# Attention decode step with gradients: pair sums and q and mod matmuls spread over even and odd heads, eight rows of sixteen scaled by ScalarE

## The chip, the cores and the metric

The kernel runs on one core of one Trainium2 chip. The core has four engines that matter here, each with its own instruction stream executed in order: TensorE (PE, with its weight loads shown as PEld), VectorE (DVE), ScalarE (ACT) and GpSimd (POOL); SyncE (SP) and POOL issue the DMAs. The metric is the device time of one execution in microseconds, the median of several runs.

## The reference, cut to what matters

One token goes through a transformer block whose layer norms are modulated by a condition vector `c`, and all gradients are taken. The part that the change touches is the forward attention: 32 heads, each with its own K and V cache of 8192 rows of 192 values.

```python
mod = (_silu(c) @ w_mod).reshape(c.shape[0], 6, 1, -1)
sa, ca, ga, sb, cb, gb = (mod[:, 0].copy(), ..., mod[:, 5].copy())
h = _layernorm(x, axis=-1) * (1 + ca) + sa
...
q = (x @ wq).reshape(B, Sq, Hq, Dh)                       # one query, 32 heads, Dh = 192
scores = jnp.einsum('bhqd,bhkd->bhqk', q, k) * Dh ** (-0.5)
p = _softmax(scores, axis=-1)
o = jnp.einsum('bhqk,bhkd->bhqd', p, v)
return o.reshape(B, Sq, Hq * Dh) @ wo
...
x = x + ga * _A_ref(h, ...)
h = _layernorm(x, axis=-1) * (1 + cb) + sb
x = x + gb * _B_ref(h, ...)                               # a small MLP mixer
```

The outputs are `x` and the gradients with respect to the inputs, among them dK and dV of the full size of the caches (out_2 and out_3), dwq and dwo, and dw_mod.

## The kernel before, in words

The kernel has a forward half and a backward half. The forward half reads K and V of all heads once and computes, besides the attention output, the products that the backward half needs; the backward half reads V again and writes dK and dV. The order of instructions on PE, DVE, ACT and SP is written out by hand (`manual_schedule` over `ORDER`): each engine executes in the order of the source.

**Tiles.** A head's 8192 rows lie on 128 partitions with 64 rows each (`J`). A K or V half (32 rows a partition, 128 x 32 x 192 bf16) is one DMA of 1536 KB. Five K buffers (`KB`) and three V buffers (`VB`) turn round. A quarter has `JQ` = 16 rows a partition.

**The loop** over heads `i` = 0 to 30 is a pipeline of three heads: `x` is head i (its scores), `y` is head i-1 (softmax, scaling of V, most matmuls), `z` is head i-2 (its last quarter and its results). In one turn the code does, in this order:

- DVE finishes the scores of the head before (`dot_sum` of `d1`, L312, and a maximum, L516), then multiplies the first K half by q (`dot_mul`, L297, tile `prod`, one buffer). PE spreads the maximum (`mx`, L520, pool `psB`, one buffer) and executes quarter 3 of `z` (`m_quarter`: lines 378 and 383 into `mp`, line 395 into `op`).
- DVE makes `negm` (L526). ACT computes the exponentials `E4` (L343) and two copies of them (L344, L346).
- DVE halves `prod` by adding its halves (`dot_half`, L302); PE sums the rest (`dot_tree`, L308, tile `dot_ps`).
- Two quarters of V are scaled by the exponentials (`scale_v`). Of the 16 rows of a quarter, DVE scales the first `JQ - NVA` in one operation (L356) and ACT the other `NVA`, one operation each (L363), after a copy of the weights into the last columns (L354). `NVA` is 7. The scaled quarter `vs` has three buffers. PE executes quarters 0 and 1 of `y`.
- Between them ACT takes the results of `z` out of PSUM (`m_out`): `M1` (L414), `mt` (L416) and `osb` (L422).
- In odd turns, PE makes the sums over partitions for the two heads of a pair (`pair_sums`, L432 to L434, fp32 matmuls of one column into `po`, pool `psS`, one buffer) before quarter 1. In turns with i % 4 = 3 it makes the first half of the next four heads' q too (`q_half`, L265, and the copy by ACT, L267).
- DVE multiplies the second K half (L297), adds `mt` (`m_add`, L427), in odd turns makes the normalised output of the pair (`pair_o`, L444 to L448), halves the product, and PE sums it (`dot_tree`).
- Quarter 2 is scaled. In odd turns PE multiplies the pair's output by `wo` (`pair_ao`, L455) and ACT copies the result (`AO`, L557); with i % 4 = 3 the second half of q follows, with i % 4 = 1 the columns of `mod` (`mod_blocks`, L241, ACT L242), as long as there are any. Then PE executes quarter 2, and quarter 3 is scaled.

**Loads.** SP issues each load when its buffer comes free: the next head's K halves after quarters 3 and 1 of earlier heads (L338), V halves after the scaling of a V half (L292), `wo` in odd turns (L211), and w_q (i % 4 = 2) and w_mod (i = 0, 4, 8) into one buffer `w_st` (L205).

The last two heads (lines 594 to 757) have their own code: scores in quarters, the loads of B_w3 and B_w4 (`w4a`, L658), the results of the last pairs, the layer norms and the MLP. The backward half starts after that.

Of the kernel before, what the change touches and what calls it, by code (L numbers as in the profile page):

```python
# [8 lines left out]
FP32 = mybir.dt.float32  # L9
# [11 lines left out]
def kernel(  # L21
# [27 lines left out]
    P = 128  # L49
    D = A_x.shape[-1]  # L50
    _, HQ, S, DH = A_k_cache.shape
# [3 lines left out]
    J = S // P  # L55
    JH = J // 2
    JQ = J // 4
# [9 lines left out]
    MW = DH + 1  # L67
# [5 lines left out]
    V_, A_, T_ = nc.vector, nc.scalar, nc.tensor  # L73
# [9 lines left out]
    psS = ctx.enter_context(tc.tile_pool(name="psS", bufs=1, space=PS))  # L83
# [150 lines left out]

    mod = col(NMB, "mod")

    def mod_blocks(b0, nb, w):
        ps = psS.tile([P, 16], FP32, name="mod_ps", tag="s")
        for b in range(nb):
            for k in range(ND):  # L240
                T_.matmul(ps[:, b : b + 1], lhsT=w[:, k, b * P : (b + 1) * P], rhs=sc_bf[:, k : k + 1], start=(k == 0), stop=(k == ND - 1))  # L241
        A_.copy(out=mod[:, b0 : b0 + nb], in_=ps[:, 0:nb])  # L242

    sa, ca, ga, sb, cb, gb = (mod[:, k * ND : (k + 1) * ND] for k in range(6))
# [4 lines left out]
    nc.sync.dma_start(out=wm_b, in_=wm_v[:, :, 9 * P : 12 * P])  # L249
    MB0 = 12  # L250
    n0, r0 = layernorm(x_c, "ln0")
    mod_blocks(0, 9, wm_a)
    mod_blocks(9, 3, wm_b)
    ha = col(ND, "ha")
    V_.scalar_tensor_tensor(out=ha, in0=ca, scalar=1.0, in1=n0, op0=ALU.add, op1=ALU.mult)
    V_.tensor_tensor(out=ha, in0=ha, in1=sa, op=ALU.add)
# [2 lines left out]

    qs_bc = const.tile([P, QD], BF16, name="qs_bc")  # L260

    def q_half(n, b, w):
        ps = psB.tile([P, 512], FP32, name="q_ps", tag="b")
        for k in range(ND):
            T_.matmul(ps[:, 0:PW], lhsT=ha_bf[:, k : k + 1].to_broadcast([P, P]), rhs=w[:, k, b * PW : (b + 1) * PW], start=(k == 0), stop=(k == ND - 1))  # L265
        lo = n * CW + b * PW
        A_.activation(out=qs_bc[:, lo : lo + PW], in_=ps[:, 0:PW], func=ACT.Copy, scale=SCALE)  # L267

# [22 lines left out]
    def load_v(h, t, v):  # L291
        nc.sync.dma_start(out=v, in_=V_hd[h][:, t * JH : (t + 1) * JH, :])  # L292
        return v

    def dot_mul(src, vec):
        prod = pp.tile([P, JH, DH], BF16, name="prod", tag="prod")
        V_.tensor_tensor(out=prod, in0=src, in1=vec[:, None, :].to_broadcast([P, JH, DH]), op=ALU.mult)  # L297
        return prod

    def dot_half(prod):  # L300
        w = DH // 2
        V_.tensor_tensor(out=prod[:, :, 0:w], in0=prod[:, :, 0:w], in1=prod[:, :, w : 2 * w], op=ALU.add)  # L302

    def dot_tree(prod, psR, w):

        ps = psR.tile([P, JH, TS], FP32, name="dot_ps", tag="d")
        for k in range(0, w, TS):
            T_.matmul(ps, lhsT=ident_bf, rhs=prod[:, :, k : k + TS], start=(k == 0), stop=(k == w - TS))  # L308
        return ps

    def dot_sum(ps, dst):
        V_.reduce_sum(out=dst, in_=ps, axis=AX.X)  # L312
# [7 lines left out]
    KX, KY, KC, KD, KE = (KB[(2 * HQ + k) % NKB] for k in (-4, -5, -3, -2, -1))  # L320
    OB = (VB[1], KY, KE, VB[1], KD)
    OR = (KY, KC, KE, KX, KD)
    NVA = (7 * JQ) // 16
    MO = 256

    def e_rows(t, pool=psS, tag="s"):
# [6 lines left out]
    with tc.tile_pool(name="vs", bufs=3) as vsp, tc.tile_pool(name="ft", bufs=2) as ft, \  # L333
            tc.tile_pool(name="psM", bufs=2, space=PS) as psM, tc.tile_pool(name="psO", bufs=2, space=PS) as psO, \
            tc.tile_pool(name="psR", bufs=2, space=PS) as psR:
        def load_k(h, t):
            kb = KB[(2 * h + t) % NKB]
            nc.sync.dma_start(out=kb, in_=K_hd[h][:, t * JH : (t + 1) * JH, :])  # L338
            return kb
# [68 lines left out]
        def o_out(h, op, es, os_):  # L408
            os_[h] = ft.tile([P, MW], FP32, name="osb")
            A_.activation(out=os_[h][:, DH:MW], in_=es, func=ACT.Copy, scale=32.0)  # L410
            A_.copy(out=os_[h][:, 0:DH], in_=op[:, 0:DH])
# [13 lines left out]
        def m_add(h, mp, mt):  # L425
            t, b = divmod(h, 2)
            V_.tensor_tensor(out=M2[64 * b : 64 * b + 64, t, :], in0=mp[0:64, MO : MO + MW], in1=mt[64:128, :], op=ALU.add)  # L427

        def pair_sum(po, b, os_h):
            rows = slice(64 * b, 64 * b + 64)  # L430
            for k in range(3):
                T_.matmul(po[rows, k : k + 1], lhsT=os_h[:, k:DH:3], rhs=c32[:, 0:1], start=True, stop=True)  # L432
            T_.matmul(po[rows, 3:4], lhsT=c32[:, 0:64], rhs=os_h[:, DH:MW], start=True, stop=True)
            T_.matmul(po[:, 4 + b : 5 + b], lhsT=c32, rhs=os_h[:, DH:MW], start=True, stop=True)  # L434

        def pair_sums(os2):
            po = psS.tile([P, 8], FP32, name="po", tag="s")
            for b in range(2):
                pair_sum(po, b, os2[b])
            return po  # L440

        def pair_o(t, po):
            rz = tcol(3, "rz")
# [7 lines left out]
        def pair_ao(o2, wo_t, pool=psS, tag="s"):  # L451
            ps = pool.tile([P, ND, 2], FP32, name="ao_ps", tag=tag)
            for i in range(ND):
                for k in range(3):
                    T_.matmul(ps[:, i, :], lhsT=wo_t[:, k, i * P : (i + 1) * P], rhs=o2[:, k, :], start=(k == 0), stop=(k == 2))  # L455
            return ps

        w = load_w(wq_v, 0, CW)
        for b in range(2):
            q_half(0, b, w)  # L460
        mb = MB0
        X, os_, wo_l = {0: {"k": [load_k(0, 0), load_k(0, 1)], "v": [load_v(0, 0, VB[0])]}}, {}, {}
        wo_l[0] = load_wo(0)
# [39 lines left out]
        with tc.manual_schedule(engines=ORDER):  # L503
            for i in range(H1):
# [32 lines left out]
                if z is not None:  # L537
                    mt = m_out(i - 2, z["mp"], z["op"], os_)
                early(i, "mid")
                if last:  # L540
                    po = pair_sums((os_.pop(i - 3), os_.pop(i - 2)))
                if i % 4 == 3 and wch is not None:
                    q_half((i + 1) // 4, 0, wch)
                if y is not None:
                    m_quarter(1, y["k"][0], vs1, y["mp"], y["op"])
                nx["k"].append(load_k(i + 1, 1))
                pb = dot_mul(x["k"][1], qh)
                if z is not None:
                    m_add(i - 2, z["mp"], mt)
                if last:  # L550
                    o2 = pair_o(t, po)
                dot_half(pb)
                x["d1"] = dot_tree(pb, psR, DH // 2)
                if y is not None:
                    vs = scale_v(2, y["v"][1], E4, Ef)
                if last:
                    A_.copy(out=AO[:, :, 2 * t : 2 * t + 2], in_=pair_ao(o2, wo_l.pop(t)))  # L557
                if i % 4 == 3 and wch is not None:
                    q_half((i + 1) // 4, 1, wch)
                    wch = None  # L560
                if i % 4 == 1 and wch is not None:
                    mod_blocks(mb, nb, wch)
                    mb += nb
                    wch = None
                if i % 2 == 1:
# [8 lines left out]
                dot_sum(x["d0"], x["S"][:, 0:JH])  # L574
                if y is not None:
                    y["vs"] = scale_v(3, y["v"][1], E4, Ef)
                nx["v"].append(load_v(i + 1, 0, VB[(2 * i + 2) % NVB]))
                early(i, "end")
                if i == H1 - 3:
# [5 lines left out]
                    nc.sync.dma_start(out=w4b[:, 5 * D : 6 * D], in_=w4v[:, 3, :])  # L585
                if i > H1 - 3:
                    dg_part(1)
                if i == H1 - 1:
                    po = psS.tile([P, 8], FP32, name="po", tag="s")
                    pair_sum(po, 0, os_.pop(H1 - 3))  # L590
            assert mb == NMB and wch is None


# [29 lines left out]
            def psr(shape, dtype, name):  # L623
                return psR.tile(shape, dtype, name=name, tag="d")
# [25 lines left out]
            score_tree(0, d1)  # L650
            score_mul(1, 1)
            score_tree(1, d1)
            dot_sum(d0, x["S"][:, 0:JH])
            m_add(H1 - 2, z["mp"], mt)
            o_rows(H1 - 1, vy, op_y, JH, J)
            o_out(H1 - 1, op_y, es, os_)
            w4a = pp.tile([P, 8, D], BF16, name="w4a", tag="prod")
            nc.sync.dma_start(out=w4a, in_=w4v[:, 4:12, :])  # L658
            w3v = [flat(VB[0])[:, k * F : (k + 1) * F] for k in range(4)] + [w3_4]
# [15 lines left out]

            dot_sum(d1, x["S"][:, JH:J])
            mx = row_max(x["S"])
            po_x = psr([P, 8], FP32, "po_x")
            pair_sum(po_x, 0, os_.pop(H1 - 1))
            negm = neg_max(mx)  # L680
            A_.activation(out=E_all[:, H1, :], in_=x["S"], func=ACT.Exp, bias=negm[:, 0:1], scale=1.0)
            op_x = psO.tile([P, 256], FP32, name="op")
            o_rows(H1, x["v"], op_x, 0, J)
            es = e_sum(H1)
            dg_part(1)
            o_out(H1, op_x, es, os_)
            pair_sum(po, 1, os_.pop(H1 - 2))
            o2 = pair_o(TL - 1, po)
            pair_sum(po_x, 1, os_.pop(H1))
            er_t = [e_rows(TL, psB, "b")]  # L690
            ps_ao = pair_ao(o2, wo_l[TL - 1])
            w3t(1)
            o2 = pair_o(TL, po_x)
            A_.copy(out=AO[:, :, 2 * TL - 2 : 2 * TL], in_=ps_ao)
            ps_ao = pair_ao(o2, wo_l[TL], psB, "b")
            aoP = col(ND, "aoP")
            V_.reduce_sum(out=aoP, in_=AO[:, :, 0 : 2 * TL], axis=AX.X)
# [613 lines left out]
```

## Time and profile before

| | us |
|---|---|
| median of 4 runs | 1445.66 |
| lowest and highest run | 1439.58, 1450.1 |
| the profiled execution | 1450.1 |
| its span, first to last instruction | 1448.3 |
| PE, DVE, ACT, POOL busy in the span | 1205.7, 1109.7, 882.4, 138.1 |
| mean granted TensorE clock | 0.715 |
| HBM read and written | 343.58 MB, 225.91 MB |

An engine's busy time is the union of its instructions. The granted clock is the share of TensorE's full clock that the throttle let through. In the forward half (about the first 570 us) it is near 1, and in the backward half 0.55 on average. DMA engines are busy nearly everywhere: the mean over the span is 395 GB/s. A wait is listed as the waiting engine, its line, the releaser, the sum in us, the count and the longest. In the timeline a row is start, duration (us), engine, line, operation, tiles and shapes, count, and in brackets the engine's idle time before it with the releaser.

### The profile page before, as it was taken

To read this page: it belongs to the slowest core of one execution; us is meant where nothing else is said; L and a number is where in the kernel's file an instruction comes from. 1 tells how busy PE (TensorE), PEld (TensorE's weight loads), DVE (VectorE), ACT (ScalarE), POOL (GpSimd) and SP (SyncE) were. 2 spreads that over 40 slices of the span, in tenths; PEclk is the share of its full clock that TensorE was granted. 3 is DMA by queue.
4 is the path that set the end of the run, shared out by engine and by line. 5 is a ranking of instruction groups with operands and counts; after the bars stand their busy time and mean duration, and the time that the engine had idled before them with its cause. 6 is when DMAs were issued, how large, how long until landed. Compare 5 with 4: busy or idle time off the path is not lost.

```text
span 1448.3 us, 29963 instructions
## 1 busy us (share of the span) xinstructions
PE 1205.7 (83%) x12577; PEld 785.7 (54%) x12577; DVE 1109.7 (77%) x1395; ACT 882.4 (61%) x1923; POOL 138.1 (10%) x240
## 2 busy tenths in 40 slices
PE   3999999999999987887888888789887788778884
PEld 1677777777777766544444444444444444444542
DVE  4999999999999996676766676776676676667674
ACT  0777766777777773545555555566566555555654
POOL 0000000000000000121110110111111111111111
PEclk9999999999999997656555555565556555555555
DMA  9999999999999995699999999999999999999997
GB/s 375 404 407 419 408 418 404 401 400 394 403 396 402 412 413 216 232 401 425 420 395 412 417 398 407 412 415 419 395 423 423 396 417 405 403 384 408 391 401 324
DMA packets 77748, 571.96 MB, mean 395 GB/s; under 512 B 8590, under 2 KB 26718, under 8 KB 37294
## 3 DMA queue, kind: packets, MB, share of 16 engines
q1 hardware_dynamic: 51402, 343.59, 58.9%
q0 software_dynamic: 26192, 226.47, 38.0%
q8 instruction: 98, 1.61, 0.4%
q14 instruction: 36, 0.29, 0.0%
q10 hardware_dynamic: 20, 0.00, 0.0%
HBM read 343.58 MB, written 225.91 MB: 393 GB/s over the span
## 4 chain that ended last, share of the span: by engine, by line
PE 38%; DVE 29%; ACT 11%; DMA 11%; issue 9%; POOL 1%; SPq 0%; ACTq 0%; POOLq 0%; DVEq 0%
PE dot_ps L938 16%; DVE prod L297 9%; DMA out_dram<-KB 6%; PE dv_ps L949 6%; DVE pq L929 5%; ACT vs L363 4%; DVE prod L302 4%; PE wT_ps L816 4%; DVE vs L356 3%; PE mp L378 3%; PE dot_ps L308 2%; DVE S_h L312 2%; ACT wT L817 2%; DMA KB<-in_A_k_cache_dram 2%; DMA out_dram<-stg 1%
## 5 line engine op out<-in xcount | busy, mean ns | idle before, releaser
L950 ACT CAST KB<-dv_ps 128x768 bf16<-128x768 f32 x504 | 382.8, 804 | 279.5 <-PE dv_ps L949 278.7
L938 PE MATMUL dot_ps<-pq,ident_bf 128*128 128x256 bf16 x1536 | 363.8, 407 | 63.5 <-DVE pq L929 63.2
L363 ACT ACTIVATE vs<-VB,Ef 128x192 bf16<-128x192 bf16 x840 | 303.2, 442 | 0.0
L938 PEld LDWEIGHTS <-ident_bf 128*128 128x128 bf16 x1536 | 190.1, 135 | 190.7 <-issue 127.9
L949 PE MATMUL dv_ps<-do_r,er_b 1*128 1x192 bf16 x2048 | 223.3, 337 | 56.1 <-ACT KB L950 51.3
L954 DVE TENSOR_TENSOR KB<-qs_bc,dS 128x3072 bf16<-128x3072 bf16 x126 | 220.4, 1750 | 26.2 <-DMA out_dram<-KB 25.8
L929 DVE TENSOR_TENSOR pq<-VB,do_r 128x3072 bf16<-128x3072 bf16 x126 | 220.4, 1749 | 0.0
L297 DVE TENSOR_TENSOR prod<-KB,qs_bc 128x6144 bf16<-128x6144 bf16 x62 | 207.8, 3351 | 9.7 <-DMA KB<-in_A_k_cache_dram 5.2
L949 PEld LDWEIGHTS <-er_b 1*128 1x128 bf16 x2048 | 92.9, 112 | 178.0 <-issue 170.2
L378 PE MATMUL mp<-vs,KB 128*128 128x193 bf16 x1920 | 187.5, 251 | 0.0
L378 PEld LDWEIGHTS <-KB 128*128 128x128 bf16 x1920 | 168.6, 100 | 17.3 <-issue 4.5
L312 DVE TENSOR_REDUCE dP<-dot_ps 128x32 f32<-128x512 f32 x64 | 44.2, 691 | 145.8 <-PE dot_ps L938 145.8
L793 POOL DMA_DIRECT2D er_b<-er_t x64 | 40.9, 639 | 1169.2 <-PE w3T_ps L666 576.4
L308 PE MATMUL dot_ps<-prod,ident_bf 128*128 128x512 bf16 x372 | 94.3, 391 | 45.7 <-DVE prod L302 45.7
L356 DVE TENSOR_TENSOR vs<-VB,E 128x1728 bf16<-128x1728 bf16 x120 | 123.5, 1049 | 0.0
L302 DVE TENSOR_TENSOR prod<-prod 128x3072 bf16<-128x3072 bf16 x62 | 108.6, 1752 | 0.6
L817 ACT COPY wT<-wT_ps 128x1024 bf16<-128x1024 bf16 x84 | 80.8, 962 | 45.1 <-PE wT_ps L816 42.0
L383 PE MATMUL mp<-vs,KB 128*64 128x193 bf16 x1920 | 103.0, 250 | 0.0
L383 PEld LDWEIGHTS <-KB 128*64 128x64 bf16 x1920 | 77.0, 109 | 19.6 <-issue 19.6
L308 PEld LDWEIGHTS <-ident_bf 128*128 128x128 bf16 x372 | 34.7, 99 | 87.2 <-issue 59.2
L1187 POOL DMA_DIRECT2D out_dram<-KB x127 | 68.4, 542 | 42.7 <-ACT KB L950 17.9
L343 ACT ACTIVATE E<-S_h,negm 128x256 bf16<-128x256 f32 x30 | 15.2, 508 | 86.5 <-DVE negm L526 86.5
(333 smaller groups left out, 1020.9 us busy)
## 6 DMA issues: line engine op xcount, KB each, us to landing
VB<-in_A_v_cache_dram SPq DMA_DIRECT2D x125, 1536.0 KB, 11.2
out_dram<-KB POOLq DMA_DIRECT2D x125, 1536.0 KB, 15.0
KB<-in_A_k_cache_dram SPq DMA_DIRECT2D x64, 1536.0 KB, 10.4
wo_st<-in_A_wo_dram SPq DMA_DIRECT2D x30, 480.0 KB, 9.1
w_st<-in_A_wq_dram SPq DMA_DIRECT2D x12, 960.0 KB, 13.4
out_dram<-wo_st POOLq DMA_DIRECT2D x16, 480.0 KB, 19.9
out_dram<-w_st POOLq DMA_DIRECT2D x7, 960.0 KB, 22.8
w_st<-in_w_mod_dram SPq DMA_DIRECT2D x6, 960.0 KB, 20.3
```

The source lines that it names most:

```text
L297: V_.tensor_tensor(out=prod, in0=src, in1=vec[:, None, :].to_broadcast([P, JH, DH]), op=ALU.mult)
L302: V_.tensor_tensor(out=prod[:, :, 0:w], in0=prod[:, :, 0:w], in1=prod[:, :, w : 2 * w], op=ALU.add)
L308: T_.matmul(ps, lhsT=ident_bf, rhs=prod[:, :, k : k + TS], start=(k == 0), stop=(k == w - TS))
L356: V_.tensor_tensor(out=vs[:, 0:n, 0:DH].rearrange("p j (a b) -> p j a b", b=4), in0=v[:, v0 : v0 + n, :].rearrange("p j (a b) -> p j a b", ...
L363: A_.activation(out=vs[:, k, 0:DH], in_=v[:, v0 + k, :], func=ACT.Copy, scale=Ef[:, j0 + k : j0 + k + 1])
L378: T_.matmul(mp[:, 0:MW], lhsT=kb[:, j0 + k, 0:P], rhs=vs[:, k, 0:MW], start=(q == 0 and k == 0), stop=(z and k == JQ - 1), skip_group_chec ...
L383: T_.matmul(mp[p0 : p0 + 64, MO : MO + MW], lhsT=kb[:, j0 + k, P:DH], rhs=vs[:, k, 0:MW], start=False, stop=(z and k >= JQ - 2), skip_grou ...
L929: V_.tensor_tensor(out=pq[:, q], in0=v_l[s][:, q * JQ : (q + 1) * JQ, :], in1=do_of(ht(s)[0])[:, None, :].to_broadcast([P, JQ, DH]), op=AL ...
L938: T_.matmul(ps[:, q * JQ : (q + 1) * JQ, :], lhsT=ident_bf, rhs=pq[:, q, :, k : k + TS], start=(k == 0), stop=(k == DH - TS), skip_group_c ...
L949: T_.matmul(ps[:, b, k * DH : (k + 1) * DH], lhsT=er[p0 : p0 + 1, 2 * m + k, :], rhs=doh[p0 : p0 + 1, :], start=True, stop=True)
L950: A_.copy(out=dV4[:, 2 * q : 2 * q + 2, m * PW : (m + 1) * PW], in_=ps[:, :, 0:PW])
L954: V_.tensor_tensor(out=dK[:, lo:hi, :].rearrange("p j (a b) -> p j a b", b=4), in0=qh.rearrange("p (a b) -> p a b", b=4)[:, None, :, :].to ...
```

## The change

`NVA` becomes 8: ACT scales eight rows of each quarter, and DVE eight (nine before). The pair sum of a head is executed once per head, after quarter 1 of the turn, and written into spare columns (200 to 207) of the `op` tile of the pair's odd head, in place of a tile of its own; in odd turns `pair_o` moves behind `dot_half` and `dot_tree`. The first half of q is made in turns with i % 4 = 3 as before but later, the second half in turns with i % 4 = 0, and mod in turns with i % 4 = 2 (1 before). The matmuls of `pair_ao`, q and mod stay before quarter 2, and ACT's copies of their results are put in a list `late` that is executed after quarter 3 has been scaled. In the last two heads, pair sums, `pair_o`, `pair_ao` and the copy of `AO` for the last pair but one come earlier or later, as the diff shows.

```diff
-    def mod_blocks(b0, nb, w):
+    def mod_mm(nb, w):
         ps = psS.tile([P, 16], FP32, name="mod_ps", tag="s")
...
+        return ps
+
+    def mod_out(b0, nb, ps):
         A_.copy(out=mod[:, b0 : b0 + nb], in_=ps[:, 0:nb])
...
-    def q_half(n, b, w):
+    def q_mm(b, w):
         ps = psB.tile([P, 512], FP32, name="q_ps", tag="b")
...
+        return ps
+
+    def q_out(n, b, ps):
         lo = n * CW + b * PW
         A_.activation(out=qs_bc[:, lo : lo + PW], in_=ps[:, 0:PW], func=ACT.Copy, scale=SCALE)
...
-    NVA = (7 * JQ) // 16
+    NVA = JQ // 2
...
-        def pair_sum(po, b, os_h):
+        def pair_sum(po, b, os_h, start=True):
             rows = slice(64 * b, 64 * b + 64)
             for k in range(3):
-                T_.matmul(po[rows, k : k + 1], lhsT=os_h[:, k:DH:3], rhs=c32[:, 0:1], start=True, stop=True)
+                T_.matmul(po[rows, k : k + 1], lhsT=os_h[:, k:DH:3], rhs=c32[:, 0:1], start=start, stop=start, skip_group_check=True)
...
                 early(i, "mid")
-                if last:
-                    po = pair_sums((os_.pop(i - 3), os_.pop(i - 2)))
-                if i % 4 == 3 and wch is not None:
-                    q_half((i + 1) // 4, 0, wch)
                 if y is not None:
                     m_quarter(1, y["k"][0], vs1, y["mp"], y["op"])
                 nx["k"].append(load_k(i + 1, 1))
+                if z is not None:
+                    po = (z if last else y)["op"][:, 200:208]
+                    pair_sum(po, i % 2, os_.pop(i - 2), start=False)
+                late = []
                 pb = dot_mul(x["k"][1], qh)
                 if z is not None:
                     m_add(i - 2, z["mp"], mt)
+                dot_half(pb)
+                x["d1"] = dot_tree(pb, psR, DH // 2)
                 if last:
                     o2 = pair_o(t, po)
-                dot_half(pb)
-                x["d1"] = dot_tree(pb, psR, DH // 2)
                 if y is not None:
                     vs = scale_v(2, y["v"][1], E4, Ef)
                 if last:
-                    A_.copy(out=AO[:, :, 2 * t : 2 * t + 2], in_=pair_ao(o2, wo_l.pop(t)))
+                    ps_ao = pair_ao(o2, wo_l.pop(t))
+                    late.append(lambda ps=ps_ao, t=t: A_.copy(out=AO[:, :, 2 * t : 2 * t + 2], in_=ps))
                 if i % 4 == 3 and wch is not None:
-                    q_half((i + 1) // 4, 1, wch)
+                    late.append(lambda ps=q_mm(0, wch), n=(i + 1) // 4: q_out(n, 0, ps))
+                if i % 4 == 0 and wch is not None:
+                    late.append(lambda ps=q_mm(1, wch), n=i // 4: q_out(n, 1, ps))
                     wch = None
-                if i % 4 == 1 and wch is not None:
-                    mod_blocks(mb, nb, wch)
+                if i % 4 == 2 and wch is not None:
+                    late.append(lambda ps=mod_mm(nb, wch), lo=mb, n=nb: mod_out(lo, n, ps))
                     mb += nb
                     wch = None
...
                     y["vs"] = scale_v(3, y["v"][1], E4, Ef)
+                for f in late:
+                    f()
                 nx["v"].append(load_v(i + 1, 0, VB[(2 * i + 2) % NVB]))
...
-                if i == H1 - 1:
-                    po = psS.tile([P, 8], FP32, name="po", tag="s")
-                    pair_sum(po, 0, os_.pop(H1 - 3))
...
             score_tree(1, d1)
+            pair_sum(po, 1, os_.pop(H1 - 2), start=False)
             dot_sum(d0, x["S"][:, 0:JH])
             m_add(H1 - 2, z["mp"], mt)
-            o_rows(H1 - 1, vy, op_y, JH, J)
-            o_out(H1 - 1, op_y, es, os_)
...
             mx = row_max(x["S"])
-            po_x = psr([P, 8], FP32, "po_x")
-            pair_sum(po_x, 0, os_.pop(H1 - 1))
+            o_rows(H1 - 1, vy, op_y, JH, J)
+            o2 = pair_o(TL - 1, po)
             negm = neg_max(mx)
             A_.activation(out=E_all[:, H1, :], in_=x["S"], func=ACT.Exp, bias=negm[:, 0:1], scale=1.0)
+            o_out(H1 - 1, op_y, es, os_)
+            ps_ao = pair_ao(o2, wo_l[TL - 1])
+            A_.copy(out=AO[:, :, 2 * TL - 2 : 2 * TL], in_=ps_ao)
+            po_x = psr([P, 8], FP32, "po_x")
             op_x = psO.tile([P, 256], FP32, name="op")
             o_rows(H1, x["v"], op_x, 0, J)
...
             o_out(H1, op_x, es, os_)
-            pair_sum(po, 1, os_.pop(H1 - 2))
-            o2 = pair_o(TL - 1, po)
+            pair_sum(po_x, 0, os_.pop(H1 - 1))
             pair_sum(po_x, 1, os_.pop(H1))
...
-            ps_ao = pair_ao(o2, wo_l[TL - 1])
             w3t(1)
             o2 = pair_o(TL, po_x)
-            A_.copy(out=AO[:, :, 2 * TL - 2 : 2 * TL], in_=ps_ao)
             ps_ao = pair_ao(o2, wo_l[TL], psB, "b")
```

More of the change, by code (lines that the diff above doesn't have):

```diff
@@ L251 @@
     n0, r0 = layernorm(x_c, "ln0")
-    mod_blocks(0, 9, wm_a)
-    mod_blocks(9, 3, wm_b)
+    mod_out(0, 9, mod_mm(9, wm_a))
+    mod_out(9, 3, mod_mm(3, wm_b))
     ha = col(ND, "ha")
@@ L427, in m_add @@
             V_.tensor_tensor(out=M2[64 * b : 64 * b + 64, t, :], in0=mp[0:64, MO : MO + MW], in1=mt[64:128, :], op=ALU.add)
-        def pair_sum(po, b, os_h):
+        def pair_sum(po, b, os_h, start=True):
             rows = slice(64 * b, 64 * b + 64)
             for k in range(3):
[L432 to L436, printed above, removed]
-            po = psS.tile([P, 8], FP32, name="po", tag="s")
-            for b in range(2):
-                pair_sum(po, b, os2[b])
-            return po
+                T_.matmul(po[rows, k : k + 1], lhsT=os_h[:, k:DH:3], rhs=c32[:, 0:1], start=start, stop=start, skip_group_check=True)
+            T_.matmul(po[rows, 3:4], lhsT=c32[:, 0:64], rhs=os_h[:, DH:MW], start=start, stop=start, skip_group_check=True)
+            T_.matmul(po[:, 4 + b : 5 + b], lhsT=c32, rhs=os_h[:, DH:MW], start=start, stop=start, skip_group_check=True)
         def pair_o(t, po):
@@ L459 @@
         for b in range(2):
-            q_half(0, b, w)
+            q_out(0, b, q_mm(b, w))
         mb = MB0
@@ L587 @@
                     dg_part(1)
-                if i == H1 - 1:
-                    po = psS.tile([P, 8], FP32, name="po", tag="s")
-                    pair_sum(po, 0, os_.pop(H1 - 3))
             assert mb == NMB and wch is None
```

## The prediction

> **What bounds the kernel now.** I first read busy time by stretch. Columns: stretch; its length; busy us of PE, PEld, DVE, ACT, POOL, with instruction counts; granted PE clock; DMA share; GB/s.
>
> ```profile
> 108.00:180.00 72.00, 67.21 (x988) 52.13 (x988) 67.24 (x62) 53.12 (x169) 0.00 (x0) 0.98 1.01 413
> 324.00:396.00 72.00, 66.40 (x956) 51.23 (x957) 67.99 (x64) 51.55 (x164) 0.00 (x0) 0.98 1.00 397
> 600.00:1448.00 848.00, 677.14 (x5039) 381.61 (x5034) 569.87 (x778) 487.41 (x703) 132.07 (x225) 0.55 0.99 403
> ```
>
> The change touches only the forward half (up to about 570 us). There DVE is busy 94% of the time, PE 92 to 93%, ACT 72 to 74%, and the DMA engines always have packets, so at least three resources stand close together. The waits of 72 to 500 us (25 heads) say who sets the pace:
>
> ```profile
> ACT E L343 <- DVE negm L526: 58.3, 25, 4.3
> ACT AO L557 <- PE ao_ps L455: 32.4, 13, 4.6
> ACT qs_bc L267 <- PE q_ps L265: 23.1, 14, 3.1
> DVE rz L444 <- PE po L434: 12.9, 13, 1.2
> DVE S_h L312 <- PE dot_ps L308: 6.3, 6, 1.4
> ```
>
> ACT's waits are long but mostly slack. DVE waits 19 us in all, for PE, nearly all in odd heads; for K tiles it waits 0.3 us. So DVE leads, and loses time to PE in odd heads.
>
> The timeline gives the rest. I count from a head's first `prod` product (L297). Even head 18 starts at 321.93, odd head 19 at 337.83, head 20 at 356.90:
>
> ```profile
> 331.82 0.32 ACT L416 COPY mt<-mp 64x193 f32<-64x193 f32 x1
> 332.38 0.35 DVE L427 TENSOR_TENSOR M<-mp,mt 64x193 f32<-64x193 f32 x1
> 332.76 1.76 DVE L302 TENSOR_TENSOR prod<-prod 128x3072 bf16<-128x3072 bf16 x1
> 333.41 0.52 PE L395 MATMUL op<-vs,ones_bf 128*32 128x193 bf16 x16
> 335.09 2.53 ACT L363 ACTIVATE vs<-VB,Ef 128x192 bf16<-128x192 bf16 x7
> ...
> 347.07 0.69 PE L432 MATMUL po<-c,osb 128*64 128x1 f32 x6
> 349.77 0.18 DVE L444 RECIPROCAL rz<-po 128x3 f32<-128x3 f32 x1 [1.14 <-PE po L434]
> 356.04 0.69 DVE L312 TENSOR_REDUCE S_h<-dot_ps 128x32 f32<-128x512 f32 x1 [1.43 <-PE dot_ps L308]
> ```
>
> Head 18 takes 15.90 us and DVE never stops. Head 19 takes 19.07: DVE waits for both pair sums (1.14), then for a dot tree (1.43) that PE reached late. Heads 18 to 21 take 15.90 + 19.07 + 16.15 + 17.36 = 68.48 us; heads 2 to 29, seven such fours, 477.9.
>
> The late PE is partly a slow PE. Six odd heads (3, 7, 13, 17, 19, 23) hold a stretch like the second line here:
>
> ```profile
> 345.80:349.20 3.40, 3.16 (x53) 2.71 (x51) 2.80 (x2) 2.54 (x8) 0.00 (x0) 1.00 1.04 435
> 349.20:352.60 3.40, 3.40 (x17) 2.46 (x17) 2.79 (x6) 1.21 (x4) 0.00 (x0) 0.50 1.00 417
> ```
>
> The granted clock is 0.50 for 3.4 us, right after a stretch with both pair sums in it. Heads 17 and 13 (half clock) take 18.17, their like without it 17.36; heads 3, 7, 19, 23 take 19.0 to 19.1, their like 17.43 to 17.51. That is 0.8 or 1.6 us an event, 8 us together.
>
> **The change, part by part.**
>
> *One row of 16 from DVE to ACT.* DVE's products cost 1751 ns for 3072 elements and 3351 for 6144: 0.521 ns an element. The quarter's product shrinks from 1728 to 1536 elements, from 1049 to 949 ns: 0.10 us a quarter, 0.40 a head, 12 us over 120 quarters. ACT adds a row: seven take 2.53 us and one alone 0.44, so 0.35 a row, 1.40 a head. The bounds of an added row are 0.35 (queued) and 0.44 (alone); I take 0.35, since the rows are queued.
>
> ACT looks free, but one point is not. DVE's `m_add` (L427) waits for ACT's copy `mt`, which stands behind the first two quarters. In head 18 `mt` is done at +10.21 and DVE's own product before `m_add` at +10.42, so the cover is 0.21. Now `mt` comes 2 x 0.35 later, at +10.91, and DVE is 0.20 earlier, at +10.22. DVE stands still for 0.7 us, and behind `m_add` wait the halving of `prod`, the dot tree, two products and two sums. From `m_add` to the next head it takes 337.83 - 332.38 = 5.45, now 0.20 less. An even head becomes 10.94 + 5.25 = **16.19** us: 0.3 longer than today. Only two of four quarters pay back on DVE, and two rows go onto the path in full.
>
> [...]
>
> *Pair sums, one per head, after the second quarter.* Removed from odd heads: one pair sum (1.1 us of PE, 347.07 to 348.18), the wait for `osb`, and the stand in front of quarter 1. In an even head PE ends quarter 1 at 333.93, +12.0; one pair sum then ends at +13.1. DVE, which now halves `prod` first, comes for `po` at 10.94 + 0.38 + 1.68 = +13.0, so 0.1 to 0.15 of wait is left of 1.14, and the four small `pair_o` operations (0.55) stay. The dot tree follows on PE at +13.1 and takes 1.5; DVE sums it at about +16, so the 1.43 goes. An odd head becomes 16.19 + 0.55 + 0.15 = **16.9**. No stretch of 3.4 us holds two pair sums any more, so I count no half-clock events.
>
> [...]
>
> *q and mod matmuls spread; ACT's `AO`, q and mod copies moved behind the last quarter.* ACT's waits for PE (32.4 + 23.1) go, but they were slack or are priced above. New cost: at every fourth head's turn DVE's first product waits for the q copy. ACT's last quarter ends at 335.09 + 2.53 = +15.69 today, at +17.09 with four rows more; `AO` and q (0.17 and 0.49) end at +17.7. Against +16.9 that is **0.86** once in four heads. The other half of q and mod are read one or more heads later and cost nothing. The copies keep `psB` and `psS` to the head's end: the next `mx` waits for the q copy, but PE reaches it at about +18, after its own matmuls.
>
> *Loads.* SP's order is unchanged. A first K half is issued when PE ends a head's last quarter, today +3.4; ACT's later rows and PE's backlog make that +4.2 to 4.6, which leaves 11.6 to 12 us against 10.2 median (14.5 longest) to landing: hidden on average, and priced by the excess where not. Second K halves go out 4 to 5 us earlier in odd heads. V halves have more than 20 us.
>
> A four without a w_mod load moves 16 x 1.573 (1536 KB) + 2 x 0.49 + 0.98 = 27.1 MB, over 67.04 us 405 GB/s; with one, 28.1 MB, 419. The best 72 us above ran 413, where 28.1 MB take 68. Two fours have it; I add 0.5 us each.
>
> *The end of the forward half.* `pair_o`, `AO` and some matmuls change places. The chain there runs through the landing of `w4a` (issued 553.59, 11.4 us), whose issue hangs on the last score trees, which move little: zero, bounds -1 to +1.
>
> **Sum.** Four heads: 16.19 + 16.90 + 16.19 + 17.76 = 67.04. Seven: 469.3, plus 1.1 for head 29's own extras (18.50 against 17.36), plus 1.0 for loads: 471.4 against 477.9, **-6.5 us**. Half of the removed waits are eaten by the new wait for `mt`. The profiled execution took 1450.1 us (span 1448.3), so 1443.6; it was the slowest of four, whose median is 1445.66. The backward half is untouched, so I shift the median: **1439.2 us**.
>
> **Rivals.**
> - *The new waits do not bind.* If `mt` came in time, DVE alone would need 15.5 + 16.05 + 15.5 + 16.05 = 63.1, and loads would set the pace. At about 418 GB/s the fours take 64.9 (five) or 67.2 (two): 459 + 1.1 against 477.9, some -18, **1428**. Against it: ACT runs without a gap from `E` to `mt` in both heads.
> - *Nothing is left.* A row at 0.44 adds 0.18 to `mt` in each head, 0.36 to a q turn: about 1 us a four; with K half a microsecond late per four, 7 x 1.5 gives +10: **1445 to 1449**.
> - *Slower: half clock in every head.* A pair sum, a dot tree and 15 `ao` or 30 mod matmuls of one or two columns now stand together in each head. If that trips the clock as two pair sums do, 28 heads pay 0.8: +22, less 6.5, **1461**. It decides from about 17 events on (beyond 0.5%). Against it: stretches with 10 of a pair's 20 small fp32 matmuls are not followed by half clock today.
> - *It does not do what it says:* the order of the built program shows eight rows on ACT and the moves as described, so no chance is set aside.
>
> **How the numbers follow.** Forecast 0.5 (own range 1434 to 1444), rival one 0.2, two 0.18, three 0.12. The range holds the first three: 1427 to 1449. Half a per cent (7.2 us, about what a measurement can tell) lies at 1438.4: faster 0.2 and a little under half of 0.5, 0.44; same 0.43; slower 0.13.
>
> **What would show it.** Right: a new DVE wait at `m_add` for ACT's `mt` of about 0.7 us a head; even heads near 16.2, odd near 16.9, every fourth near 17.8, with a wait of the first product for the q copy; `rz` waits near 0.1; no half clock between 72 and 540 us. Wrong: no wait at `mt`; DVE waiting for K tiles more than 5 us in all; clock 0.50 in many heads.

## The result, and the profile after

The changed kernel takes 1441.92 us (median of 43 runs, 1432.17 to 1447.69) against 1446.62 for the kernel before (64 runs beside them): a ratio of 0.9966, 95% interval 0.9954 to 0.9977, or 4.9 us less (3.3 to 6.7). The forecast was 6.5 less. The profiled execution of the changed kernel took 1441.61 us, its span 1439.8.

Busy time by stretch, in the columns of the table shown for the kernel before:

```profile
108.00:180.00 72.00, 67.79 (x1012) 52.04 (x1008) 66.87 (x63) 58.46 (x187) 0.00 (x0) 0.98 1.01 417
324.00:396.00 72.00, 65.74 (x960) 50.44 (x960) 68.04 (x64) 59.72 (x190) 0.00 (x0) 1.00 1.00 406
600.00:1439.00 839.00, 679.56 (x5018) 383.94 (x5015) 567.37 (x777) 486.08 (x702) 131.57 (x224) 0.54 1.00 407
```

ACT's share rose from 72 to 74% to 81 to 83%, DVE's stayed, and the loads run at 406 to 417 GB/s (397 to 413 before). DVE's waits from 72 to 500 us (waiting line, releaser: us in total, times, longest) are of another kind than before:

```profile
DVE M L433 <- ACT mt L422: 11.6, 21, 0.7
DVE prod L303 <- DMA KB<-in_A_k_cache_dram: 5.3, 11, 1.2
DVE prod L303 <- ACT qs_bc L273: 3.1, 6, 0.6
DVE prod L303 <- PE dot_ps L314: 2.0, 2, 1.1
DVE S_h L318 <- PE dot_ps L314: 0.4, 2, 0.3
DVE rz L444 <- PE op L440: 0.4, 2, 0.2
```

Before, DVE stood 19 us for PE in odd heads. Now it stands 2.8 us for PE (2.0 of it for a dot tree, in heads 6 and 10), 11.6 us for `mt`, 5.3 for K tiles (0.3 before) and 3.1 for the q copy. In sum these waits are no shorter than before (22.8 us, 19.5 before); DVE has 0.40 us a head less to do. In the timeline of heads 18 and 19, which start at 319.89 and 336.05 (head 20 at 353.58), the wait at `m_add` is there in both:

```profile
330.81 0.35 DVE L433 TENSOR_TENSOR M<-mp,mt 64x193 f32<-64x193 f32 x1 [0.70 <-ACT mt L422]
...
346.97 0.35 DVE L433 TENSOR_TENSOR M<-mp,mt 64x193 f32<-64x193 f32 x1 [0.70 <-ACT mt L422]
349.20 0.18 DVE L444 RECIPROCAL rz<-op 128x3 f32<-128x3 f32 x1
...
353.58 3.36 DVE L303 TENSOR_TENSOR prod<-KB,qs_bc 128x6144 bf16<-128x6144 bf16 x1 [0.55 <-ACT qs_bc L273]
```

The last line is the new wait for the q copy, and `rz` no longer waits. An undisturbed even head takes 16.17 us, an odd one 16.89, an odd one with a q copy 17.53. Yet heads 2 to 29 together went only from 477.92 to 475.35: 2.6 us, where the sum had 6.5. What the heads show of the cause is in two places. One is head 29, which took 20.90 (18.50 before). Its start, at 503.96, with the half of q that PE makes just before it:

```profile
502.20 0.98 PE L268 MATMUL q_ps<-w_st,ha_bf 128*128 128x384 bf16 x5
...
505.69 0.28 PE L174 MATMUL bc_t<-ident_f,dbo 128*5 128x128 f32 x1
...
506.00 0.26 ACT L176 CAST bc_rows<-bc_t 5x128 bf16<-5x128 f32 x1 [0.78 <-PE bc_t L174]
...
507.92 0.80 PE L520 MATMUL mx<-ident_f,m 128*128 128x128 f32 x2 [0.35 <-ACT w4b L182]
...
508.76 0.29 DVE L526 TENSOR_REDUCE negm<-mx 128x1 f32<-128x128 f32 x1 [1.45 <-PE mx L520]
...
513.98 3.36 DVE L303 TENSOR_TENSOR prod<-KB,qs_bc 128x6144 bf16<-128x6144 bf16 x1 [1.53 <-PE dot_ps L314]
```

Between turns 28 and 29 stands the broadcast of `dbo` (`bcast_cols`, L174 to L182): a transpose, a copy by ACT, matmuls, a copy, a matmul, a copy, PE and ACT in turn. It stands ahead of `mx`, so when it is late, DVE stands still twice. Its transpose starts 1.73 us into head 29; in the kernel before, where head 29 starts at 508.31, it was 0.72:

```profile
509.03 0.27 PE L174 MATMUL bc_t<-ident_f,dbo 128*5 128x128 f32 x1
```

What is late is PE: from 494.4 to 505.9, in turn 28, it now runs without a listed pause, since a pair sum (1.1 us) and half of q (0.98) have come into that turn. ACT is not what holds the broadcast up: it waits 0.78 us for the transpose, and in the order alone (below), with seven rows, 1.91, where the transpose still starts at +1.78. The other place is the heads around the w_mod loads (5, 6, 9 and 10, each 0.4 to 0.8 us longer than their like) and head 23 (0.7), where K comes late; in heads 6 and 10 a half-clock stretch follows.

The rest of the 8.5 us between the two spans was not traced to the change. The first product of the backward half comes 2.2 us earlier; beyond it the two executions differ in waits such as this one, of before and then of after:

```profile
DVE KB L954 <- DMA out_dram<-KB: 25.8, 10, 4.7
```

```profile
DVE KB L956 <- DMA out_dram<-KB: 8.5, 3, 4.1
```

The diff does not touch that code, and it varies from run to run: in the experiments, the profiled executions of the order alone and of the copies at once differ by 2 us in heads 2 to 29 and by over 9 in their spans (1433.1 and 1442.6). So I judge steps by the heads and totals by the medians.

### The profile page after: what moved, and what is told of

The parts are those of the page before. It is cut to its first block, busy times and chain, and to the rows that moved or that the text cites. A ratio compares the mean times of both kernels' runs of the same rounds, so it can differ in the third digit from the quotient of the medians.

```text
span 1439.8 us, 30112 instructions
## 1 busy us (share of the span) xinstructions
PE 1208.1 (84%) x12577; PEld 786.7 (55%) x12577; DVE 1098.7 (76%) x1395; ACT 920.1 (64%) x2043; POOL 138.2 (10%) x240
## 4 chain that ended last, share of the span: by engine, by line
PE 39%; DVE 24%; ACT 18%; DMA 10%; issue 8%; POOL 1%; SPq 0%; ACTq 0%; POOLq 0%; DVEq 0%
PE dot_ps L940 19%; ACT vs L369 10%; PE dv_ps L951 7%; DVE prod L303 6%; DVE pq L931 5%; DMA KB<-in_A_k_cache_dram 5%; PE wT_ps L818 5%; PE mp L384 2%; DVE prod L308 2%; DMA er_b<-er_t 2%; ACT wT L819 2%; PE dot_ps L314 2%; ACT KB L952 2%; DVE vs L362 2%; DVE S_h L318 1%
## 5 line engine op out<-in xcount | busy, mean ns | idle before, releaser
L369 ACT ACTIVATE vs<-VB,Ef 128x192 bf16<-128x192 bf16 x960 | 344.6, 443 | 0.0
L940 PEld LDWEIGHTS <-ident_bf 128*128 128x128 bf16 x1536 | 190.0, 135 | 182.2 <-issue 119.4
L303 DVE TENSOR_TENSOR prod<-KB,qs_bc 128x6144 bf16<-128x6144 bf16 x62 | 207.9, 3353 | 21.2 <-DMA KB<-in_A_k_cache_dram 10.3
L384 PEld LDWEIGHTS <-KB 128*128 128x128 bf16 x1920 | 165.0, 98 | 17.0 <-issue 5.9
L362 DVE TENSOR_TENSOR vs<-VB,E 128x1536 bf16<-128x1536 bf16 x120 | 111.6, 950 | 0.0
L389 PEld LDWEIGHTS <-KB 128*64 128x64 bf16 x1920 | 77.2, 110 | 19.6 <-issue 19.6
L314 PEld LDWEIGHTS <-ident_bf 128*128 128x128 bf16 x372 | 39.1, 106 | 89.3 <-issue 58.8
```

The lines of the kernel that those rows point to most:

```text
L362: V_.tensor_tensor(out=vs[:, 0:n, 0:DH].rearrange("p j (a b) -> p j a b", b=4), in0=v[:, v0 : v0 + n, :].rearrange("p j (a b) -> p j a b", ...
L369: A_.activation(out=vs[:, k, 0:DH], in_=v[:, v0 + k, :], func=ACT.Copy, scale=Ef[:, j0 + k : j0 + k + 1])
L384: T_.matmul(mp[:, 0:MW], lhsT=kb[:, j0 + k, 0:P], rhs=vs[:, k, 0:MW], start=(q == 0 and k == 0), stop=(z and k == JQ - 1), skip_group_chec ...
L389: T_.matmul(mp[p0 : p0 + 64, MO : MO + MW], lhsT=kb[:, j0 + k, P:DH], rhs=vs[:, k, 0:MW], start=False, stop=(z and k >= JQ - 2), skip_grou ...
```

## The experiments

Ratios are to the kernel before, run on the same chip; the experiments ran in three rounds on three chips, where it took 1445.2, 1447.8 and 1446.5 us, so between rounds the ratios compare better than the medians. Heads are counted from a head's first `prod` product to the next one's; "heads 2 to 29" is their sum in the profiled execution.

| run | median us | ratio, 95% | heads 2 to 29 | undisturbed even, odd |
|---|---|---|---|---|
| the change | 1441.9 | 0.9966 (0.9954 to 0.9977) | 475.4 | 16.17, 16.89 |
| order only | 1435.0 | 0.9937 (0.9914 to 0.9960) | 469.6 | 15.90, 17.09 |
| row only | 1459.9 | 1.0121 (1.0081 to 1.0161) | 494.9 | 16.2, 17.9 to 18.1 |
| `m_add` late | 1438.0 | 0.9962 (0.9936 to 0.9988) | 471.3 | 15.63, 16.90 |
| rows 7, 7, 8, 8 | 1434.2 | 0.9926 (0.9899 to 0.9952) | 470.4 | 15.70, 16.90 |
| rows 8, 8, 7, 7 | 1439.6 | 0.9957 (0.9929 to 0.9986) | 472.7 | 16.37, 17.09 |
| pairs together | 1445.3 | 0.9980 (0.9955 to 1.0005) | 479.7 | 15.90, 18.14 |
| copies at once | 1435.2 | 0.9910 (0.9879 to 0.9941) | 471.6 | 15.90, 17.09 |
| 7, 7, 8, 8, light loads | 1425.6 | 0.9849 (0.9812 to 0.9886) | 461.1 | 15.70, 16.90 |

### Which half of the change does what: the order alone, the row alone

The order alone is the changed kernel with

```diff
-    NVA = JQ // 2
+    NVA = (7 * JQ) // 16
```

> The changed kernel with seven rows on ACT again (NVA = 7), so the new order alone. My theory: the eighth row sits on the path from E over two quarters to mt and m_add, so without it the wait at m_add goes (mt at +10.2, DVE's product at +10.4). Even heads 15.90, odd heads 10.83 + 1.67 + about 0.65 of wait for po + 0.55 + 3.40 = 17.1, no wait for the q copy (ACT ends at +16.3): 66.0 us for four heads against 67.1. Seven fours would bring 7 to 8 us against the changed kernel, of which later K loads (411 GB/s) take back some 2 to 4: 1436 to 1439 us, 0.5 to 0.7% below the kernel before. Rival, the row pays (DVE's 0.4 us a head is what counts): slower than the changed kernel by up to 12 us, 1450 or more. Rival, loads already set the pace: same as the changed kernel, 1442, with the wait moved to K tiles.

Four heads take 65.99 us, the forecast 66.0; there is no half clock between 72 and 550 us, and 1435.0 in all. The row alone is the kernel before with the opposite edit:

> The kernel before with NVA = 8 alone. My theory: mt comes 0.70 us later, even heads 16.2; in odd heads osb comes 0.7 later too, so the second pair sum, po and rz: about 18.0 and 19.7 instead of 17.4 and 19.05. Four heads 70.1 against 68.3, seven fours +13 us: 1456 to 1460 us, 0.7 to 0.9% slower than the kernel before. Rival, the row pays on DVE: 0.4 us a head faster, about 1435. Rival, ACT's row is hidden and DVE is not the bound: 1446, no change.

It costs 1.2%. DVE's `m_add` waits for `mt` 13.8 us in 24 heads, and seven odd heads fall into half clock and take 18.8 to 21.2 us. (Its profiled execution, of 1474.3 us, is the slowest of six, so its heads are long beside the median.) So the order is what makes the change faster, and the row takes part of it back: 5.7 us in heads 2 to 29, while the intervals of the two totals just overlap.

### The wait for `mt`: its place, and the rows ahead of it

`m_add` behind the dot tree, where `mt` has long come:

```diff
-                if z is not None:
-                    m_add(i - 2, z["mp"], mt)
                 dot_half(pb)
                 x["d1"] = dot_tree(pb, psR, DH // 2)
+                if z is not None:
+                    m_add(i - 2, z["mp"], mt)
```

> The changed kernel (eight rows) with m_add moved behind dot_half and dot_tree, so that DVE halves prod while ACT still makes mt. My theory: the 0.7 us wait at m_add goes; even heads 15.5, odd heads are held by po at about 16.9, every fourth by the q copy at 17.5: 65.4 us for four heads against 67.1, 12 us in all if loads could follow (415 GB/s), which they can only partly: 1434 to 1438 us. Rival, the wait for mt is a symptom and ACT's total is the bound: no change, 1442. Rival, loads set the pace: the m_add wait is replaced by waits of prod (L303) for K tiles of the same sum, 1441 to 1442.

The wait is gone and even heads fall to 15.63, but odd heads stay at 16.90: DVE now comes earlier for `po` (the pair sum), and `rz` waits 6.6 us where it waited 0.4. Heads 7, 8, 11 and 12 take 16.9 to 18.3 with late K, and heads 2 to 29 end 4 us below the change. The next two keep `m_add` and move rows between the quarters ahead of `mt` and those behind it:

```diff
-        def scale_v(q, v, E4, Ef, n=JQ - NVA):
+        def scale_v(q, v, E4, Ef):
+            n = JQ - NVA + (q < 2)
```

> The changed kernel with seven rows on ACT in quarters 0 and 1 (before mt) and eight in quarters 2 and 3 (behind mt). My theory: only rows in front of mt cost; mt at +10.2 and no wait, even heads 15.7, odd heads held by po at 16.9, q turns 16.9 to 17.0: 65.2 us for four heads, as good as or better than the order alone: 1434 to 1438 us. Rival, the count of rows matters and not their place: half way between the changed kernel and the order alone. Rival, loads set the pace: equal to the order alone within 0.2%.

and `(q >= 2)` in place of `(q < 2)`:

> The mirror of the 7-7-8-8 kernel: eight rows on ACT in quarters 0 and 1 (before mt), seven in quarters 2 and 3. The number of rows is the same, only their place differs. My theory: mt at +10.9 holds m_add for 0.7 us in each head and nothing is paid back behind it: even heads 10.94 + 5.45 = 16.4, odd heads 17.1, 67.0 us for four heads: 1441 to 1445 us, 0.4 to 0.7% slower than 7-7-8-8 (1434) and no better than the changed kernel with eight everywhere. Rival, the count of rows decides: equal to 7-7-8-8. Rival, loads decide: equal to 7-7-8-8 too.

Both give ACT 30 rows a head. With 7, 7, 8, 8 an even head takes 15.70 and no wait for `mt` is left; with 8, 8, 7, 7 it takes 16.37, and the wait is larger than in the change:

```profile
DVE M L434 <- ACT mt L423: 13.6, 21, 0.7
```

So in the heads it is not the count of rows on ACT that costs, but the two rows that stand ahead of `mt`, and those in even heads alone: 15.90 becomes 16.37, and 15.70 becomes 16.17. Odd heads do not change by them (17.09 and 17.09, 16.90 and 16.89), since there DVE waits for the pair sum behind `m_add` in any case. The two rows behind `mt` pay back on DVE in full, 0.20 a head, in both kinds. The totals point the same way, but their intervals overlap.

### The pair sums, and the copies

The order alone, with both pair sums in the odd turn, still behind quarter 1:

```diff
-                if z is not None:
+                if last or i == H1 - 1:
                     po = (z if last else y)["op"][:, 200:208]
+                    if last:
+                        pair_sum(po, 0, os_.pop(i - 3), start=False)
                     pair_sum(po, i % 2, os_.pop(i - 2), start=False)
```

> The order-only kernel (seven rows) with both pair sums of a pair in the odd turn again, one after the other behind quarter 1. My theory: the second pair sum lies between quarter 1 and DVE's rz: PE ends it at +14.2 and not +13.1, odd heads 18.2 and not 17.1, even heads unchanged: +2.2 us for four heads, +15 us: about 1450 us, back above the kernel before; and stretches at half clock come back behind the 20 small matmuls, 0.8 us or more each where they fall, up to 1458. Rival, the spread of the pair sums is worth little, since PE has slack: within 3 us of the order-only kernel. On the clock alone: with my reading several stretches at 0.50 between 72 and 500 us, with the rival reading (only idle time halves the clock) none.

The wait for both sums is back in every odd head, which takes 18.14 (forecast 18.2):

```profile
DVE rz L444 <- PE op L440: 19.5, 13, 1.6
```

But from 72 to 500 us there is no half clock at all:

```profile
72.00:500.00 428.00, 388.37 (x5743) 301.50 (x5742) 404.95 (x390) 309.08 (x982) 0.00 (x0) 1.00 1.00 406
```

So the total came out below my expectation, at 1445.3: spreading the sums is worth about 1 us an odd head in waiting, but "two pair sums in a stretch trip the clock" is wrong. The last part of the order, ACT's copies of `AO`, q and mod made at once again:

```diff
-                    late.append(lambda ps=ps_ao, t=t: A_.copy(out=AO[:, :, 2 * t : 2 * t + 2], in_=ps))
+                    A_.copy(out=AO[:, :, 2 * t : 2 * t + 2], in_=ps_ao)
...
-                    late.append(lambda ps=q_mm(0, wch), n=(i + 1) // 4: q_out(n, 0, ps))
+                    q_out((i + 1) // 4, 0, q_mm(0, wch))
```

> The order-only kernel (seven rows) with ACT's copies of AO, q and mod made right after their matmuls and not in the late list, so ACT stands before quarter 3 until PE has them. My theory: with seven rows ACT's stand is slack (its last quarter ends at +18.0 to +18.8 in the head, the next E comes at +3.6 of the next head, which is +20.7): no change, within 0.15% of the order-only kernel (1435), and no wait of DVE for the q copy at all. Rival, freeing ACT is what the order gains: 5 to 10 us slower, 1440 to 1445.

ACT waits 22.6 us for `AO` and 22.7 for q, where the order alone has 1.6 for q, and undisturbed fours take 65.98 as they did: those waits were slack, and the list `late` is worth nothing that these runs can tell.

### Late loads, and head 29

Half of each V half is loaded for heads 2 to 29; the other rows keep what an earlier head left, so the output is of other data. First with rows 7, 7, 8, 8:

```diff
+        if not 2 <= h <= 29:
+            return load_v(h, t, v)
+        nc.sync.dma_start(out=v[:, 0:JQ, :], in_=V_hd[h][:, t * JH : t * JH + JQ, :])
```

> The 7-7-8-8 kernel with half of each V half loaded in the loop for heads 2 to 29 (the other rows keep what an earlier head left, so the attention's V products are of other data). Loads shrink by 44 MB, the instructions stay. My theory: the waits of prod for K tiles (7.1 us in 72 to 500) go and the fours with w_mod become like the others, 15.7 + 16.9 + 15.7 + 16.9 = 65.2: heads 2 to 29 take 460 to 462 us and not 470, the execution 9 to 11 us less, 1423 to 1426. Rival, the K waits come from late issue and not from the amount of data: 1431 to 1434, K waits as before.

```profile
72.00:500.00 428.00, 403.38 (x5957) 311.88 (x5955) 415.24 (x403) 339.75 (x1079) 0.00 (x0) 1.00 0.86 324
```

The last column is 324 GB/s where the full loads ran 414. No wait for K is left, and undisturbed fours take 65.2: 9 us go, more than the 7.1 that DVE had waited for K. Head 29 still took 21.17. The same loads on the change itself:

> The changed kernel itself with half of each V half loaded for heads 2 to 29 (the other rows keep what an earlier head left, so the outputs are of other data). It prices what loads that come late cost the change as it stands. Theory (the waits for K and the low clock behind them are the second part that my sum lacked, some 3 to 4 us in heads 2 to 28): no wait for K, every even head 16.2, odd heads 16.9 and 17.5, heads 2 to 28 together 450.4 us and 2 to 29 471.3, total about 1438. Rival (the low clock stretches are of the order of the matmuls and not of late loads): heads of 17 to 18 us stay where the clock is low, 1441 to 1442. Head 29 stays at about 20.9 in both.

1437.7 us, ratio 0.9936 (0.9914 to 0.9959). No K wait, no half clock, every head at 16.2, 16.9 or 17.5, and heads 2 to 28 take 451.0 (forecast 450.4) against 454.45: late K costs the change 3.4 us. The part on head 29 missed: it took 19.35, not 20.9, and here its half-clock stretch is absent. (In the five kernels of the new order, the broadcast not spread, that have such a stretch about 4 us into head 29, it takes 20.8 to 21.3 us; in the three with no half clock in it, 19.3 to 19.6.) Last, the broadcast spread: its transpose at the end of turn 28, its matmuls inside turn 29, `dg_part` of turns 29 and 30 both in turn 30.

```diff
+                if i == H1 - 2:
+                    b1 = psS.tile([P, P], FP32, name="bc_p1", tag="s")
+                    T_.matmul(b1, lhsT=pick(ND, 4), rhs=bc_rows[0:ND, :], start=True, stop=True)
...
+                if i == H1 - 2:
+                    b0 = psB.tile([P, 512], FP32, name="bc_ps", tag="b")
+                    for b in range(4):
+                        T_.matmul(b0[:, b * P : (b + 1) * P], lhsT=pick(ND, b), rhs=bc_rows[0:ND, :], start=True, stop=True)
+                    late.append(lambda: A_.copy(out=dbo_bc[:, 0 : 4 * P], in_=b0))
...
-                    bcast_cols(dbo, ND, dbo_bc, A_.copy)
...
-                if i > H1 - 3:
-                    dg_part(1)
+                if i > H1 - 2:
+                    dg_part(2)
```

> The changed kernel, with the broadcast of dbo no longer one ping-pong of TensorE and ScalarE between turns 28 and 29: its transpose stands at the end of turn 28 with its copy behind the other late copies, its five matmuls inside turn 29, and the two dg_part of turns 29 and 30 both in turn 30. Theory (the broadcast, which now stands behind ScalarE's later copies, holds up the row maximum of turn 29 and costs head 29 the 2.9 us that my sum does not have): E of turn 29 at about +3.6 instead of +5.1, no wait of pb for the dot tree, head 29 at 16.9 instead of 20.9 (0.9 of it is the dg_part that only moved to turn 30), heads 2 to 30 together 3 us shorter, total about 1439. Rival (head 29 is long because its K and V come late or because TensorE's clock is low there whatever the order): head 29 keeps 19 us or more after the 0.9 is taken off, total unchanged at 1442.

Head 29, which starts here at 502.99, has its `negm` without a wait and its exponentials at +3.58, not +5.13:

```profile
504.82 0.39 PE L520 MATMUL mx<-ident_f,m 128*128 128x128 f32 x2
...
506.25 0.28 DVE L526 TENSOR_REDUCE negm<-mx 128x1 f32<-128x128 f32 x1
...
506.57 0.51 ACT L349 ACTIVATE E<-S_h,negm 128x256 bf16<-128x256 f32 x1 [1.29 <-DVE negm L526]
```

Heads 29 and 30 take 17.06 + 17.79 = 34.85 against 20.90 + 16.91 = 37.81: 2.96 us, as the theory said. That the broadcast ahead of `mx` is what costs is so shown; that ACT's later copies hold it up, as the theory also has it, is not so: it is PE, as the rows of head 29 above show. In all 1436.8, ratio 0.9930 (0.9901 to 0.9960), 5 us below the change, of which 3 are accounted for; the intervals overlap. The same on two other orders:

> The version with rows 7, 7, 8, 8 and the broadcast spread in the same way: the two corrections that the runs point to, together. Theory: head 29 goes from 20.9 to 16.9 (0.9 of it moved to turn 30), the rest as with rows 7, 7, 8, 8 alone: 1434.2 less 3, so 1431. Rival (the time won is lost again to K that comes late, since the loads set the pace in this version): 1434, with more waits for K in turns 29 and 30.

> The order alone (7 rows in every quarter) with the broadcast spread. Its head 29 took 19.6 instead of 17.1. Theory: head 29 goes to about 17.1, of which 0.9 moved to turn 30, so 1435.0 less 1.6, about 1433.4. Rival as in the run before: 1435.

In their heads 29 and 30 it took away 3.0 and 1.5 us. In the totals nothing of it can be seen: 1435.8 (0.9916, 0.9889 to 0.9942) and 1437.5 (0.9924, 0.9894 to 0.9954), against 1434.2 and 1435.0 without it. Part of the first was given back at once (head 31's first product starts 4.3 us earlier, its third 3.2, after a wait for K of 1.1 us); the rest lies within the intervals. Rows 7, 7, 8, 8, the order alone and their spread forms all stand at 1434 to 1438: all ahead of the kernel before, and these runs do not rank them.

## Why the prediction was right, and where its sum was not

**What bounds the kernel: right.** DVE leads, and lost its time to PE in odd heads. With the row kept off ACT's early quarters and the loads lightened, DVE alone sets the even head's 15.70; in the odd head's 16.90 it still waits 0.55 us for the pair sum (`rz`, 6.6 us in 12 heads).

**The row and `mt`: right, to the hundredth.** `mt` was done at +10.89 (10.91 forecast), the wait was 0.70, the even head 16.17 (16.19). The runs with rows 7, 7, 8, 8 and 8, 8, 7, 7 show in the heads that the place makes the price, and the row alone costs 1.2%. Per quarter the added row takes 0.34 us on ACT (2.87 against 2.53) and spares DVE 0.10 (950 against 1049 ns). With the order of before that is a loss (the row alone, 1459.9), but rows moved to ACT behind `mt` cost nothing that can be told (1434.2 with 7, 7, 8, 8 against 1435.0 with seven in all).

**Pair sums: right in waiting and in effect.** Odd heads took 16.89 (16.9), and `rz` waits 0.4 us in all. In the change no half-clock stretch follows a pair sum. The reason given for that was wrong: both sums in one stretch are not enough for it, since they stood together again in a run without half clock (pairs together, 1.00 from 72 to 500 us). That the half-clock events were rightly left out of the sum is in that part luck.

**The q copy: over-estimated.** 0.86 was forecast at every fourth head; it is about 0.6, and the head 17.53, not 17.76: 7 x 0.23 = 1.6 us less than forecast. ACT's last quarter ended at +17.06 (17.09 forecast), but `AO` and q added 0.44 and not 0.66, since the records of successive ACT operations overlap (`AO` 353.01 to 353.16, q from 353.06).

**The loads: under-estimated.** They were priced at 1.0 in all. Taking them away is worth 3.4 in heads 2 to 28. The fours with a w_mod load do not just wait 0.5 for K: in heads 6 and 10 the first product waits 0.34 and 0.67, a half-clock stretch begins 5.3 to 5.4 us into the head, and the second product waits 0.98 and 1.07 more for the dot tree. With light loads the waits and these stretches are gone; but K that came 1.24 late at head 24 had no such stretch behind it. The prediction named "DVE waiting for K tiles more than 5 us in all" as a sign against it, and 5.3 it was.

**Head 29: the step that failed in size.** "1.1 for head 29's own extras" was taken as unchanged, 18.0 in all; it was 20.90. The diff does not touch the broadcast between turns 28 and 29, but PE reaches it 1.0 us later, behind the pair sum and the half of q that came into turn 28. Of that half the prediction said that it would "cost nothing", looking only at when its result is read, and not at what stands behind it in PE's queue. Without half clock the late broadcast costs some 1.4 us (19.35 and 19.6 where that stretch is absent), with it 2.9.

**The sum.** Heads 2 to 28 were forecast at 452.4 + 1.0 = 453.4 and took 454.45: +2.4 for loads, -1.6 for q, +0.3 for the rest. Head 29 adds 2.9. That is the 3.9 us between -6.5 and -2.6. The end of the forward half was put at zero, and the first backward product kept 2.2 of the 2.6. The medians show -4.9, with an interval from -6.7 to -3.3, between the two: by them the sum is too large by 1.6, by the profiled pair by 3.9. Which of the two is nearer for the heads alone can't be settled from one profile of each. But the 2.2 to 2.6 us that the traces show in the forward half lie below that interval, so the mechanism as traced does not account for the whole gain of the medians, and that the total came so near the forecast is in part luck; where the rest comes from stays open.

**Rivals.** "The new waits do not bind" fell by 11.6 us at `mt`. "Nothing is left" had K half a microsecond late in every four; it was so only in the early ones and in head 23. "Half clock in every head" had its point at 17 events; three came, none at a pair sum.

## What to carry to other kernels

When work moves to an engine with free time, ask which of its results another engine takes next, and put the added work behind that result: here 30 rows a head cost or paid by their quarter alone. When an order shifts an engine's queue by a microsecond, walk also through the one-off pieces at the edges of the loop that the diff leaves alone: one of them, between two turns, took back half of the forecast gain. And once the compute engines are faster, price loads by the stretch that has most of them, together with what follows a late one: here, in heads 6 and 10, half clock and a wait of 0.98 and 1.07 us for the dot tree, and neither with light loads.

## What the runs showed of the hardware

**When the clock is halved.** In the loop of the change half clock came in three stretches of 3.41 us, at 122.1, 190.4 and 507.8; their starts are 20 and 93 times 3.41 us apart. "PE busy" of the profile does not tell when it comes:

```profile
118.70:122.10 3.40, 1.36 (x34) 1.05 (x34) 3.40 (x4) 1.77 (x7) 0.00 (x0) 1.00 0.98 409
122.10:125.50 3.40, 3.40 (x13) 1.80 (x12) 2.42 (x3) 3.40 (x11) 0.00 (x0) 0.50 1.04 433
```

Here, in the change, a stretch with PE busy 1.36 of 3.40 is followed by half clock; in the kernel before it was one with 3.16, while one of the change at 528.3, with 1.57, has full clock behind it. Of those 3.16, the pair sums' share is this (the same stretch of the kernel before, `po` alone):

```profile
345.80:349.20 3.40, 1.89 (x19) 1.78 (x19) 0.00 (x0) 1.00 1.04 435
```

Nineteen matmuls of one column each fill 1.89 us. With both pair sums together in the odd turn, one behind the other from 316.07, the clock is 1.00 in the stretch at 315.8 and in the one behind it; there the dot tree's matmuls start at 318.09, right behind the sums, where the kernel before had a wait of 0.24 us for `osb` between the two. Whether that is the difference, and why six odd heads of fourteen were hit before and the others not, these runs do not show.

**A row in the queue.** Eight rows of 192 elements on ACT take 2.87 us, seven 2.53: 0.34 for the added one, though one alone is shown with 0.44.
